# The second chunk's values ahead of five weight pieces, and the broadcast of the maxima moved to SyncE's queue

## The chip, the cores and the metric

The kernel runs on one core of a Trainium2 chip. The metric is device time in microseconds (us), taken on the core. A core has TensorE (PE, matrix products), VectorE (DVE), ScalarE (ACT), GpSimd (POOL) and SyncE (SP); SP, ACT and POOL can issue DMA transfers, and 16 DMA engines carry them. Each engine works through its own instructions in order and waits on semaphores for the others.

## The reference

An mLSTM cell over 4 batches x 8 heads, 768 steps, head width 40, and behind it a feed-forward block with 2048 hidden units:

```python
for t in range(S):
    m_new = np.maximum(f_gate[:, :, t] + m, i_gate[:, :, t])
    f_stab = np.exp(f_gate[:, :, t] + m - m_new)
    i_stab = np.exp(i_gate[:, :, t] - m_new)
    C = f_stab * C + i_stab * outer(vt, kt);  n = f_stab * n + i_stab * kt
    y[:, :, t] = sigmoid(o_gate[:, :, t]) * (C @ qt) / np.maximum(np.abs(n @ qt), 1.0)
x = y.transpose(0, 2, 1, 3).reshape(3072, 320)
h = x @ w_in                       # 320 x 2048
out = (h * sigmoid(1.702 * h)) @ w_out   # 2048 x 320
```

(Broadcast dimensions are shortened here.)

## The kernel before

The 768 steps are cut into six chunks of 128 steps (w = 0 to 5), and each chunk is worked in closed form: running maxima by scans on DVE (`gates`), weights between steps as exponentials on ACT (`weights`, L435), scores and values as matrix products (`scores`, `values`), and a state carried from chunk to chunk (`carry`, L596). While PE does the feed-forward block of chunk w, the attention part of chunk w+1 is put between its blocks. The order is written out by hand: the program is in manual schedule, so each engine and each DMA queue has exactly the order of the source.

The change concerns the time of chunk 0's feed-forward block (w = 0), about 25 to 110 us. These parts matter:

- *The pieces of the weights.* Both weight matrices arrive in 20 pieces of 128 x 512, 0 to 9 for w_in and 10 to 19 for w_out. `fetch(n)` (L157) issues the two or three DMAs of a piece on SP. `convert(n)` turns its bits into the form that PE reads: two activations on ACT (L243, L247) and four operations on DVE (L256, L257, L259, L265). `fetched` says at which pair of hidden blocks pieces are fetched, `converted` when they are converted: pieces 13, and 14 to 16, around the last two pairs; pieces 17, 18 and 19 at the output blocks 0, 4 and 5.
- *The up products.* `up(w, j, between)` (L608) does two of eight pairs of hidden blocks at a time, with j = 0, 2, 4, 6. ACT applies the activation (L635) to each pair, and runs the conversions between them.
- *The down products.* `down` (L753, matmuls on L758) is called in 16 blocks; the first eight use w_out's first half (pieces 10 to 14), the others the second half (pieces 15 to 19). After block 0 come `columns`, `scale` and `decay` of chunk 1, after block 1 and 3 `weights`, after block 3 `carry`, after block 6 `scores`, after blocks 8 and 9 `values`.
- *What a carry needs.* `scale` (L582, POOL) multiplies the values `v_st` of the chunk by factors in `cols` and writes `vw`; `carry` multiplies `vw` with k on PE. `cols` is filled by `columns` on ACT (L367, L371) from a small transposition on DVE (L356, `columns_turn`), which reads rows that went through DRAM (`gates`, `columns_in`).
- *The values.* `load(1, "v")` issues three DMAs on SP (L120): 320 KB and twice 160 KB, in runs of 40 numbers (160 bytes). `v_st` is one buffer, so chunk 1's values may be written only when chunk 0's were read by `values(0, 3)` and by `scale(0, 1)`.
- *The broadcast of the maxima.* `gates(1)` writes the running maxima to DRAM (`m_row`); `spread(1)` (L397) reads them back in four DMAs of 256 KB, each row spread to 64 partitions, into `wt`, where `weights` works on them. For w = 1 `side_queue` sends the small rows and this broadcast through POOL's queue, for later chunks through SP's.

A DMA of SP's queue is issued only when the one eight places before it has completed, as the program has eight semaphores in turn for them.

Of the kernel before, what the change touches and what calls it, by code (L numbers as in the profile page):

```python
# [26 lines left out]
def kernel(  # L27
# [12 lines left out]
    nc = tc.nc  # L40
# [12 lines left out]
    HL = L // 2  # L53
# [41 lines left out]
    def k_of(w):  # L95
        return (k_0, k_1)[w] if w < 2 else k_st[:, 0:BH * D].rearrange("s (h d) -> s h d", d=D)
# [13 lines left out]
    def load(w, what, bs=slice(0, B)):  # L110
        hs = slice(bs.start * H, bs.stop * H)
        for c in what:
            if c == "o" and w not in eo:
                eo[w] = ld.tile([L, BH, D], FP, tag="eo", bufs=1, name="eo")
            dst, src = {"k": (k_of(w), k), "q": (q_st, q), "v": (v_st, v), "o": (eo.get(w), o_gate)}[c]
            if w and c in "kv":
                for i, t, r in ((0, slice(0, L), slice(0, L)), (1, slice(0, HL), slice(HL, L)),
                                (1, slice(HL, L), slice(0, HL))):
                    x = src[:, :, w * L + t.start:w * L + t.stop, :].rearrange("b (p two) s d -> two s (b p) d", two=2)
                    nc.sync.dma_start(out=dst[r, i::2, 0:D], in_=x[i])  # L120
                continue
            nc.sync.dma_start(out=dst[:, hs, 0:D],
                              in_=src[bs, :, w * L:(w + 1) * L, :].rearrange("b h s d -> s (b h) d"))
# [109 lines left out]
    def convert(n):  # L233
        convert_begin(n)
        convert_end(n)
# [42 lines left out]
    def side_queue(w):  # L278

        return G if w == 1 else nc.sync  # L280
# [59 lines left out]
    def masks():  # L340
        V.tensor_reduce(out=odd, in_=full.rearrange("p (j two) -> p two j", two=2)[:, 1], axis=AX.X, op=OP.add)
        V.memset(odd[BH:2 * BH, :], 0.0)
        V.tensor_scalar(out=even, in0=odd, scalar1=-1.0, scalar2=1.0, op0=OP.mult, op1=OP.add)

    def columns_in(w):

        st_row, d_row = stacked[w]
        x = raw[w] = gate.tile([L, 5 * BH], FP, bufs=1, name="raw")
        for n in range(L // 32):
            side_queue(w).dma_start(out=x[n * 32:n * 32 + 32, 0:3 * BH].rearrange("r (k t) -> r k t", t=32),  # L350
                              in_=st_row[n].rearrange("(k r) t -> r k t", r=BH))
        side_queue(w).dma_start(out=x[:, 3 * BH:], in_=d_row.rearrange("h x -> (h x)").unsqueeze(0).to_broadcast([L, 2 * BH]))
# [44 lines left out]
    def spread(w):  # L397

        for c in range(2):
            x = wt[w, c] = work.tile([L, NJ, 2, HL], FP, tag="wt", bufs=2, name="wt")  # L400
            for n in range(2):
                src = m_row[w][n, c * PH:(c + 1) * PH].rearrange("h t -> (h t)")
                side_queue(w).dma_start(out=x[n * HL:(n + 1) * HL].rearrange("s j i t -> s (j i t)"),
                                  in_=src.unsqueeze(0).to_broadcast([HL, PH * HL]))

    p_w = {}
# [169 lines left out]
    def scale(w, c, part=0, parts=1):  # L576
        n = PH // parts
        hs = slice(c * PH + part * n, c * PH + (part + 1) * n)
        if part == 0:
            vw[w, c] = work.tile([L, PH, D1], FP, tag="u", name="vw")  # L580
        e = cols[w][:, 2 * BH + hs.start:2 * BH + hs.stop].unsqueeze(2).to_broadcast([L, n, D1])
        G.tensor_tensor(out=vw[w, c][:, part * n:(part + 1) * n], in0=v_st[:, hs, :], in1=e, op=OP.mult)  # L582

    def wait_for(x):

        G.tensor_copy(out=mark, in_=x[:, 0:1])

    def carry(w, c):
        js = slice(c * NJ, (c + 1) * NJ)
        pc = banks("p_c")  # L590
        n = 2 if 0 < w < NW - 1 else 1
        for j in range(NJ):
            for i in range(2):
                for x in range(n):
                    t = slot(i, x) if w else slice(0, L)
                    T.matmul(pc[i * 64:i * 64 + 64, x, j * D1:(j + 1) * D1], k_cols(w, t, c * PH + 2 * j + i),  # L596
                             vw[w, c][t, 2 * j + i, :], start=True, stop=True)
        new = lambda x: pc[:, x, 0:NJ * D1].rearrange("r (j d) -> r j d", d=D1)
        if w == 0:
            A.copy(out=state[1][:, js], in_=new(0))  # L600
            return
        for x, dst in enumerate((state_mid, state[1 - w % 2])[:n]):
            if x:
                decay(w, c, x, V)
            V.tensor_tensor(out=dst[:, js], in0=new(x), in1=dst[:, js], op=OP.add)
# [163 lines left out]
    def weight_sums(n):  # L769
        out, a, b = ((t1, w01, w00), (t2, w11, t1), (w01, w11, w01), (t4, w10, t2))[n]  # L770
        G.tensor_tensor(out=out, in0=a, in1=b, op=OP.subtract)
# [5 lines left out]
    def hidden_difference(w, j):  # L777

        a00, a10 = hidden(w, j, 0), hidden(w, j, 1)
        G.tensor_tensor(out=a10, in0=a00, in1=a10, op=OP.subtract)  # L780
# [51 lines left out]
    def run(calls):  # L832
        for f, *args in calls:
            f(*args)
# [47 lines left out]
    convert(2)  # L882

    converted = {0: ((3, 4), (5,)), 1: ((6,), (7, 8)), 2: ((9, 10), (11, 12)), 3: ((13,), (14, 15, None, 16))}
    fetched = {0: range(10, 18), 3: (18, 19)}

    def attention(w):
        at = (0, 1, 3, 3, 5, 6, 8, 8, 9, 12, 14) if w == 1 else (0, 0, 1, 3, 1, 4, 5, 6, 6, 10, 11)
# [9 lines left out]
    for w in range(NW):  # L898
        more = w + 1 < NW
        if w == 0:  # L900
            for j in range(NF // 2):
                if j % 2 == 0:
                    ahead, behind = converted[j // 2]
                    run([(convert, p) for p in ahead] + [(fetch, p) for p in fetched.get(j // 2, ())])
                    up(w, j, lambda: run([(columns_turn, 1) if p is None else (convert, p) for p in behind]))
                if j == 6:
                    load(1, "o")
                if j == 1:
                    wait_for(w_in_sb[:, 1, 512:1024])
                    scale(0, 1)  # L910
                if j < B and j % 2:
                    carry(0, j // 2)
                if j == 3:
                    masks()
                    gates(1)
                    columns_in(1)
                    spread(1)
                if j == 4:
                    load(1, "v")
                if j >= B:  # L920
                    transposes(1, j - B)
                if j in (4, 5):
                    block_transposes(1, 2 * j - 7)
        else:
            token_sums(w)
            if more:
                gates(w + 1)
                load(w + 1, "o")
            for j in range(NF // 2):
                up_fast(w, j)  # L930
                if w == 1 and j < 4:
                    weight_sums(j)
                if more and j == 2:
                    load(w + 1, "vk")
                    columns_in(w + 1)
                    spread(w + 1)
                if more and j:
                    for n in ((), (0, 2), (4,), (6, 1), (3,), (5, 7), ())[j - 1]:
                        block_transposes(w + 1, n)
                if more and j == 7:  # L940
                    columns_turn(w + 1)
                if 2 <= j < 6:
                    hidden_difference(w, j - 2)
                if j >= 6:
                    hidden_sums(w, (j - 6,), G)
            gelu_fast(w, NF // 2 - 1)
            hidden_sums(w, (2, 3), V)
        side = attention(w + 1) if more else {}
        if w == 0:
            block_transposes(1, 5)  # L950
            block_transposes(1, 7)

            blocks = [(lambda b=b, n=n: down(w, b, n)) for n0 in (0, 2) for b in range(B) for n in (n0, n0 + 1)]
        else:
            blocks = down_fast(w, 0) + down_fast(w, 1)
        for i, block in enumerate(blocks):
            if w == 0 and i in (0, 4, 5):
                convert((17, 18, 19)[max(i - 3, 0)])
            if w + 2 < NW and i == (6 if w == 0 else 0):
                load_gates(w + 2)  # L960
            if w + 2 < NW and i == 13:
                load_squares(w + 2, "kq" if w else "k")
            if w == 0 and i == 15:
                load_squares(w + 2, "q")
            block()
            run(side.get(i, []))
            if w == 0 and i in (11, 13):
                input_sums(slice(0, 4) if i == 11 else slice(4, 8))
# [30 lines left out]
```

## Time and profile before

| | |
|---|---|
| median of 3 runs | 468.26 us (467.49, 468.26, 473.1) |
| profiled execution, own time | 468.38 us |
| its span, first to last instruction | 466.7 us |
| PE busy | 459.5 us (98%) |
| DVE busy | 341.1 us (73%) |
| ACT busy | 189.3 us (41%) |
| POOL busy | 164.5 us (35%) |
| granted PE clock | 0.999 of full |
| DMA | 52.87 MB, 113 GB/s over the span |

A line of a timeline gives the start and the duration in us, the engine (a q behind it stands for the engine's queue of instructions, where DMAs are issued), the source line, what is written and read, the shape, and in brackets the idle time before and what ended it. A line of the waits gives the total, how often, and the longest, in us.

### The profile page before, as it was taken

How to read it: one execution, taken by the hardware profiler on the slowest of the kernel's cores; microseconds unless marked ns; L12 is line 12 of the kernel's file. 1: busy time of each engine (PE TensorE's matmuls, PEld its weight loads, DVE VectorE, ACT ScalarE, POOL GpSimd, SP SyncE). 2: the span in 40 equal slices, each digit the busy share in tenths (PEclk: the TensorE clock that was granted, in tenths of full speed). 3: DMA queues.
4: the chain of work that ended last, by engine and by line, in shares of the span. 5: the costliest groups of instructions: out<-in, count | busy, mean ns of one | idle time of the engine just before them, and what ended most of it. 6: DMA issues, size and time to landing. Idle time of an engine off the chain costs nothing.

```text
span 466.7 us, 12363 instructions
## 1 busy us (share of the span) xinstructions
PE 459.5 (98%) x5063; PEld 387.2 (83%) x5063; DVE 341.1 (73%) x699; ACT 189.3 (41%) x431; POOL 164.5 (35%) x157
## 2 busy tenths in 40 slices
PE   8999998999999999999999999999999999999997
PEld 6867875776778999678999778999878999876997
DVE  6788997789788876688875788876768867545612
ACT  5686699000536600554800453900444810254100
POOL 5101325200798600266800257610148510157100
PEclk9999999999999999999999999999999999999999
DMA  9999999038994045998024998114989305100000
GB/s 172 194 302 171 230 277 181 1 76 180 163 161 106 4 100 115 192 129 148 3 60 116 199 138 148 27 46 112 183 134 126 88 18 131 36 1 0 1 29 30
DMA packets 135561, 52.87 MB, mean 113 GB/s; under 512 B 101984, under 2 KB 131632, under 8 KB 135504
## 3 DMA queue, kind: packets, MB, share of 16 engines
q1 hardware_dynamic: 126816, 49.22, 55.9%
q10 hardware_dynamic: 8048, 1.66, 1.8%
q0 software_dynamic: 640, 1.20, 1.2%
q8 instruction: 40, 0.66, 0.6%
q14 instruction: 17, 0.14, 0.1%
HBM read 44.52 MB, written 7.54 MB: 112 GB/s over the span
## 4 chain that ended last, share of the span: by engine, by line
PE 94%; DMA 2%; DVE 1%; SPq 1%; issue 1%; POOL 0%; ACT 0%; POOLq 0%; DVEq 0%
PE p_out L812 33%; PE p_h L703 27%; PE p_h L711 8%; PE p_out L758 6%; PE p_h L620 5%; PE p_c L596 2%; DMA v_st<-in_v_dram 2%; PE p_o L503 2%; PE p_s L459 2%; PE p_i L511 2%; PE p_h L629 1%; PE p_t L386 1%; PE p_s L448 1%; SPq L120 1%; PE p_w L415 1%
## 5 line engine op out<-in xcount | busy, mean ns | idle before, releaser
L749 POOL TENSOR_TENSOR g<-g,parts 128x512 f32<-128x512 f32 x30 | 38.3, 1275 | 189.7 <-DVE parts L741 148.2
L737 ACT COPY parts<-p_h 128x256 f32<-128x256 f32 x40 | 14.9, 374 | 153.6 <-PE p_h L703 152.0
L812 PE MATMUL p_out<-w_out_sb,g 128*128 128x160 f32 x480 | 69.5, 301 | 0.0
L812 PEld LDWEIGHTS p_out<-w_out_sb,g 128*128 128x128 f32 x480 | 66.5, 190 | 0.9
L703 PE MATMUL p_h<-xT,w_in_sb 128*128 128x256 f32 x240 | 66.9, 388 | 0.0
L684 ACT ACTIVATE g<-g 128x512 f32<-128x512 f32 x80 | 50.0, 631 | 39.1 <-DVE g L744 24.5
L703 PEld LDWEIGHTS p_h<-xT,w_in_sb 128*128 128x128 f32 x240 | 43.7, 190 | 18.5 <-issue 6.7
L817 DVE TENSOR_TENSOR o_sb<-o_sb,p_out 128x160 f32<-128x160 f32 x70 | 21.4, 317 | 40.5 <-PE p_out L812 39.9
L812 PE MATMUL p_out<-t_sb,s 128*128 128x160 f32 x320 | 47.1, 300 | 0.0
L740 DVE TENSOR_TENSOR t_x<-p_h,parts 128x256 f32<-128x256 f32 x40 | 16.7, 418 | 39.0 <-PE p_h L711 34.2
L812 PEld LDWEIGHTS p_out<-t_sb,s 128*128 128x128 f32 x320 | 44.4, 190 | 0.2
L703 PE MATMUL p_h<-t_x,s_in 128*128 128x256 f32 x160 | 41.1, 379 | 0.0
L711 PE MATMUL p_h<-xT,w_in_x 64*128 64x512 f32 (+1 forms) x192 | 39.8, 540 | 0.0
L435 ACT ACTIVATE wt<-wt,cols 128x64 f32<-128x64 f32 x160 | 38.8, 333 | 0.1
L758 PE MATMUL p_out<-w_out_sb,g 128*128 128x320 f32 x128 | 35.7, 436 | 0.0
L703 PEld LDWEIGHTS p_h<-t_x,s_in 128*128 128x128 f32 x160 | 30.4, 190 | 4.1
L758 PEld LDWEIGHTS p_out<-w_out_sb,g 128*128 128x128 f32 x128 | 23.9, 190 | 9.6
L741 DVE TENSOR_TENSOR parts<-p_h,t_x 128x512 f32<-128x512 f32 x40 | 27.7, 692 | 3.5
L620 PE MATMUL p_h<-xT,w_in_sb 128*128 128x256 f32 x128 | 29.8, 385 | 0.0
L748 ACT COPY g<-p_h 128x512 f32<-128x512 f32 x30 | 17.4, 580 | 30.7 <-PE p_h L711 25.3
L711 PEld LDWEIGHTS p_h<-xT,w_in_x 64*128 64x128 f32 x192 | 16.9, 186 | 14.7 <-issue 13.5
L744 DVE TENSOR_TENSOR g<-p_h,parts 128x512 f32<-128x512 f32 x40 | 27.6, 691 | 1.4
(198 smaller groups left out, 840.1 us busy)
## 6 DMA issues: line engine op xcount, KB each, us to landing
q_sq<-in_q_dram SPq DMA_DIRECT2D x20, 320.0 KB, 10.3
k_sq<-in_k_dram SPq DMA_DIRECT2D x16, 320.0 KB, 6.4
wt<-m_row SPq DMA_DIRECT2D x16, 256.0 KB, 5.2
out_dram<-o_sb SPq DMA_DIRECT2D x24, 160.0 KB, 2.0
eo<-in_o_gate_dram SPq DMA_DIRECT2D x5, 640.0 KB, 7.5
bits<-in_moe_w_in_dram SPq DMA_DIRECT2D x6, 512.0 KB, 9.9
q_sq<-x_row SPq DMA_DIRECT2D x10, 256.0 KB, 2.9
v_st<-in_v_dram SPq DMA_DIRECT2D x14, 160.0 KB, 5.3
```

Of the source, the lines that this page charges most:

```text
L435: A.activation(out=x[:, h, :], in_=x[:, h, :], func=AF.Exp, scale=-1.0, bias=cols[w][:, c * PH + h:c * PH + h + 1])
L620: T.matmul(ph[j][i][:, t], w_in_sb[:, c, f * 128:(f + 1) * 128], x[:, c, t], start=(first and c == 0 and n == 0), stop=(not first and c == ...
L684: A.activation(out=gs[w, j][:, i, :], in_=gs[w, j][:, i, :], func=AF.Gelu_apprx_sigmoid)
L703: T.matmul(out, a, x[n], start=start, stop=stop)
L711: T.matmul(row[:, t], w_in_x[r, j, :], rest_x[r, 2, t], start=(not late and h == 0), stop=(late and h == n - 1))
L741: V.tensor_tensor(out=y[:, half_w:3 * half_w].rearrange("p (a t) -> p a t", a=2), in0=flat[:, half_w:3 * half_w].rearrange("p (a t) -> p a ...
L744: V.tensor_tensor(out=g[:, 1, :], in0=row1, in1=y[:, half_w:3 * half_w], op=OP.add)
L748: A.copy(out=g[:, 0, :], in_=row0)
L749: G.tensor_tensor(out=g0, in0=g0, in1=u, op=OP.add)
L758: T.matmul(po, gs[w, f // 2][:, f % 2, b * L:(b + 1) * L], w_out_sb[:, f, :], start=(f == 0), stop=(f == NF - 1))
L812: T.matmul(po, a(f), b[:, f, :], start=(f == 0), stop=(f == NH - 1))
L817: V.tensor_tensor(out=dst, in0=x, in1=po, op=OP.add)
```

## The change

Three edits. The load of the second chunk's values (`load(1, "v")`) is issued at j = 1, right behind `scale(0, 1)`, instead of at j = 4. Of the pieces that were fetched together at the first pair (10 to 17), pieces 13 to 17 are fetched at the second (j = 2), so that the values stand between piece 12 and piece 13 in SP's queue. The broadcast (`spread`) is issued by SP for every chunk, and for chunk 1 at j = 4 instead of j = 3; it stands in SP's queue between piece 17 and piece 18. POOL keeps the small rows of chunk 1 (`m_row`, `st_row`, `d_row`, `raw`). On PE, DVE and ACT the instructions and their order are the same.

```diff
@@ spread
-                side_queue(w).dma_start(out=x[n * HL:(n + 1) * HL].rearrange("s j i t -> s (j i t)"),
+                nc.sync.dma_start(out=x[n * HL:(n + 1) * HL].rearrange("s j i t -> s (j i t)"),
                                   in_=src.unsqueeze(0).to_broadcast([HL, PH * HL]))
@@ the order of chunk 0
-    fetched = {0: range(10, 18), 3: (18, 19)}
+    fetched = {0: range(10, 13), 1: range(13, 18), 3: (18, 19)}
...
                 if j == 1:
                     wait_for(w_in_sb[:, 1, 512:1024])
                     scale(0, 1)
+                    load(1, "v")
                 if j < B and j % 2:
                     carry(0, j // 2)
                 if j == 3:
                     masks()
                     gates(1)
                     columns_in(1)
+                if j == 4:
                     spread(1)
-                if j == 4:
-                    load(1, "v")
```

## The prediction

> **What bounds the kernel now.** I read the page first (busy times, slices), then the list of waits for the stretch that the change touches, then the chain of waits there, and last the timelines of ScalarE (ACT) and SyncE (SP).
>
> ```profile
> span 466.7 us, 12363 instructions
> ...
> PE 459.5 (98%) x5063; PEld 387.2 (83%) x5063; DVE 341.1 (73%) x699; ACT 189.3 (41%) x431; POOL 164.5 (35%) x157
> ...
> DMA  9999999038994045998024998114989305100000
> ```
>
> TensorE (PE) is busy 459.5 of 466.7 us, so no reordering can win more than the 7.2 us left, 1.5%. The first seven DMA digits are 9: up to about 80 us the DMA engines are full. There a load can only come earlier if another comes later. The waits between 58 and 95 us:
>
> ```profile
> POOL vw L582 <- DMA v_st<-in_v_dram: 11.4, 1, 11.4
> ...
> PE p_c L596 <- POOL vw L582: 2.1, 2, 1.6
> POOL wt L403 <- DMA raw<-st_row: 2.0, 1, 2.0
> ```
>
> PE loses 2.1 us here (1.57 + 0.55) before the two carries of the second chunk, because GpSimd (POOL) scales the values late, and POOL waits for the load of v. The chain, start and duration in us:
>
> ```profile
> 64.05 10.94 DMA v_st<-in_v_dram
> ...
> 75.16 0.17 POOL vw L582
> ...
> 76.44 1.74 POOL vw L582
> 78.18 0.04 issue
> 78.22 1.14 PE p_c L596 x64
> ```
>
> After 78.2 the chain is PE to the end of the kernel, so what is won or lost here reaches the end whole. The timeline of ACT shows what else a carry needs (start, duration):
>
> ```profile
> 58.95 0.70 ACT L243 ACTIVATE w_out_sb<-bits 128x512 f32<-128x512 f32 x1
> 59.54 0.68 ACT L247 ACTIVATE bits<-bits 128x512 uint32<-128x512 uint32 x1
> 60.98 1.08 ACT L635 ACTIVATE g<-p_h 128x512 f32<-128x512 f32 x2 [0.77 <-PE p_h L629]
> ...
> 69.87 0.26 ACT L367 ACTIVATE cols<-cols 128x64 f32<-128x64 f32 x1
> 70.03 0.51 ACT L371 ACTIVATE cols<-raw 64x32 f32<-64x32 f32 x2
> 70.57 0.59 ACT L435 ACTIVATE wt<-wt,cols 128x64 f32<-128x64 f32 x2
> ```
>
> 58.95 is the conversion of piece 13, the first of those that the change puts behind v. From there to the scale factors (cols, 70.13) ACT idles once, for 0.77 us. POOL's scaling reads both v and cols: v came at 74.99, cols 4.9 us before it.
>
> **The change, part by part.** (1) The three loads of v move from behind pieces 13 to 17 (12 DMAs) to in front of them. SP issued the last part of piece 12 at 49.2 and the first of piece 13 at 51.4; a DMA of SP waits for the completion of the one eight places ahead. So v is issued from 51.4 instead of 59.7. What v overwrites was last read by POOL's earlier scaling, done at 37.0, and by PE at 23.4: no new wait.
>
> When does v land? The engines are full, so it is served after piece 12, whose last part lands at 49.2 + 6.6 = 55.8. Its service time has two bounds. Low: the k load of the same shape and line (L120) landed at 43.7, behind gate rows that landed at 38.0: 5.7 us. High: v in this trace, from piece 17's landing (58.5 + 6.0 = 64.5) to 75.0, is 10.4 us, with 1 MB of broadcast reads (4 x 256 KB on POOL's queue) inside; at the 354 GB/s of the window 59 to 64 us those are 3.0 us, which leaves 7.4. I take 6.5, between 5.7 and 7.4, as the broadcast is no longer beside it: v lands at 62.3, 12.7 us earlier than now.
>
> The Trainium skill's page "DMA: Bandwidth & Descriptors" (section "Anatomy of one DMA — SWDGE (gpsimd) path") fits 2.0 us plus bytes over 436 GB/s, an estimate of 3.5 us for these 640 KB; v would land at 59.3, and the sum would be the full gain of the second case below. [...]
>
> (2) Pieces 13 to 17 come later. Piece 18 stands behind v now, in the same three parts as piece 13, and its last part lands at 71.5 + 4.8 = 76.3, 1.3 us after v. So piece 13 is complete at 62.3 + 1.3 = 63.6; today it is at 52.5 + 4.7 = 57.2, with 1.7 us in hand before ACT's 58.95. ACT now waits at the conversion until 63.6, and behind it in ACT's order stand the activations of pair 6, pieces 14 to 16, pair 7, the copies of kT, piece 17, cols, and the exponentials of L435. From 58.95 to 70.13 these are 11.18 us, less the 0.77 of idle time that the delay swallows: 10.4. For waits inside (piece 16 is issued only after v has landed, and 62.3 + 4.7 + two more parts is about 68, just when ACT gets there) I allow 0.5, between 0 and 1.5. Cols are done at 63.6 + 10.4 + 0.5 = 74.5, 4.4 later than now.
>
> (3) So POOL's scaling starts at 74.5, released by ACT instead of by v. One scaling took 1.3 us (75.16 to 76.44): the first carry can start at 75.8 instead of 76.5; PE has been ready since 74.96. The second follows as now. **Gain 0.7 of the 2.1 us.** Break-even is piece 13 at 64.3; past it each us of lateness costs one.
>
> (4) VectorE (DVE) is released by ACT's first half of piece 13, at 64.2 instead of its own 62.3. A piece takes it 2.35 us (62.27 to 64.61), so 13 and 14 are done at 68.9. PE's second output block starts at 68.4 (66.18 + 8.78/4) and reaches piece 14 half-way, at 69.5: 0.6 in hand. A stall there is the same lateness as in (3), not more, as the carry waits for cols anyway.
>
> (5) The four broadcast reads of L403 leave POOL, where they took 0.5 us each to issue while POOL had nothing else until 75.2: worth nothing. On SP they stand behind piece 17 and in front of pieces 18 and 19, o and the gates. Later chunks show them on SP: 3.05 us for four issues, 5.2 us from issue to landing. Issued at about 67 to 69, behind a full queue, they land at 72 to 74; ACT's L435 starts at 74.9. Hidden, with about 1 us of cover and more behind it (third rival). POOL's small rows keep their place, and the columns they bring are turned by DVE (69.3 now) about 2 us later, ahead of ACT's cols. Pieces 18 and 19, needed after L435 (74.9 + 7.75 = 82.7), land by about 80 with the same total traffic. Nothing is added to or removed from any engine's work.
>
> The sum goes by one profiled execution: 468.38 us, span 466.7 and 1.7 around it, 0.1 above the median of 468.26. 468.38 - 0.7 = 467.7; against the median **467.6**.
>
> **The rivals.** *The cover holds* and the stall goes whole: piece 13 complete by about 62.6, cols at 73.0, both scalings in time. 468.26 - 2.1 = 466.2. For it: with k's 5.7 us piece 13 comes at 62.8. Against it: the v row itself, and the queue that refills behind v (piece 16).
>
> *Piece 13 late, slower.* In ACT's order everything behind its conversion is late, and cols take v's place as the last thing, later than v was. It decides from 64.3. With the high bound, 10.4 us for v, piece 13 comes at 55.8 + 10.4 + 1.3 = 67.5 and cols at 77.9 to 78.4: the carry at 79.2 to 79.7, 2.7 to 3.2 later than now, 471.0 to 471.5; half-way 469.7. For it: ACT sits 4.6 us before the first w_out piece already, so these loads have no large lead, and SP's issue of v was held for 3.5 and 4.5 us. Against it: the 10.4 holds broadcast traffic that moves away.
>
> The page "TensorE: Matmul & The Clock Gate" (Part 1) says that PE's clock halves after some 3.4 us idle. The present wait of 1.57 us shows a granted clock of 1.00 in its stretch, which the page allows; a wait of 4.7 us would bring by it about 2 us more, an estimate of mine, to 473.
>
> *The broadcast late, slower.* The reads land behind pieces 13 to 17. L435 (7.75 us), two pieces on ACT and DVE and the product with the scores (1.2) must be over by PE's 92.55; the product ended at 89.9. Counting 7.75 + 0.7 + 4.9 to 6.8 + 1.2 back from 92.55, L435 must start by 76.1 to 78.0. At the longest landing on POOL's queue, 8.7 us after an issue at 69, it would start at 77.7: 0 to 1.6 lost besides the missed gain, 468.3 to 469.9. Against it: 5.2 us is the usual time.
>
> That the change does nothing, v landing at 75 again, would need v held back at issue; nothing ahead of it in SP's queue waits past 52.
>
> **How the numbers follow.** Forecast (gain 0 to 1.4) 0.43; full gain 0.22; piece 13 late 0.25; broadcast late 0.07; no effect 0.03. The likeliest gives 467.6, its own range 466.8 to 468.4. To hold 8 in 10 the range takes in the full gain with 0.2 of scatter, 466.0, and most of the late case, 471.0. A measurement of this kernel tells about 2% (9.4 us) from no change. Faster by that is more than PE's whole idle time: 0.01. Slower by it needs late pieces, a late broadcast and a slowed PE together: 0.04. Within: 0.95.
>
> **What would show it.** In the profile after: v lands near 62; POOL's wait before L582 ends by ACT's L367, not by the DMA of v; ACT has a new wait of about 4.6 us before L243, ended by the DMA of bits; L435 starts near 75; PE's wait at L596 is 0.5 to 1.5 us instead of 2.1. Wrong would be: no wait on ACT (the full gain), a wait at L758 for pieces of w_out, an L435 that waits for its broadcast, or a wait at L596 over 2.1.

## The result and the profile after

| | before | after |
|---|---|---|
| median of 20 runs each, on one chip | 468.6 us (466.26 to 473.1) | 468.1 us (466.65 to 470.55) |
| ratio after to before, 95% interval | | 0.9991 [0.9967, 1.0015] |
| profiled execution: time, span | 468.38, 466.7 us | 467.52, 465.8 us |

No change that can be measured: the medians are 0.5 us apart, and the interval reaches from 1.5 us won to 0.7 lost. The page of the changed kernel:

```profile
span 465.8 us, 12359 instructions
...
PE 459.9 (99%) x5063; PEld 387.9 (83%) x5063; DVE 340.9 (73%) x699; ACT 189.3 (41%) x431; POOL 163.9 (35%) x153
...
DMA  8999998049993036997024998024999305000000
```

The span is 0.9 us shorter, PE's busy time is the same within 0.4, and the DMA engines are full as before, up to about 80 us. The list of waits between 58 and 95 us of the changed kernel (total, how often, longest):

```profile
POOL vw L582 <- DMA wt<-m_row: 13.1, 1, 13.1
ACT w_out_sb L243 <- DMA bits<-in_moe_w_out_dram: 3.8, 1, 3.8
DVE u L517 <- PE p_i L511: 3.0, 1, 3.0
```

ACT has the new wait for piece 13 that the forecast spoke of. PE's wait before the carries (L596) is gone from the list. The name behind POOL's wait is not its cause: the scaling L582 reads `v_st` and `cols`, not the broadcast. It began when ACT had just written `cols`, as the timelines of ACT and POOL show (start, duration):

```profile
57.09 1.07 ACT L388 COPY kT<-p_t 128x512 f32<-128x512 f32 x2
61.98 0.68 ACT L243 ACTIVATE w_out_sb<-bits 128x512 f32<-128x512 f32 x1 [3.82 <-DMA bits<-in_moe_w_out_dram]
...
72.26 0.26 ACT L367 ACTIVATE cols<-cols 128x64 f32<-128x64 f32 x1
72.96 7.76 ACT L435 ACTIVATE wt<-wt,cols 128x64 f32<-128x64 f32 x32
```

```profile
72.65 2.65 POOL L582 TENSOR_TENSOR vw<-v_st,cols 128x656 f32<-128x656 f32 x2 [13.11 <-DMA wt<-m_row]
```

`cols` (L367) ends at 72.52, the scaling starts at 72.65, and both halves are done at 75.30. PE gets to the carry after that, at 75.96, as the chain of waits shows (start, duration):

```profile
67.34 8.62 PE p_out L758 x32
75.96 2.01 PE p_c L596 x128
77.96 6.66 PE p_out L758 x24
```

The carry runs without a gap. The blocks behind it start at 77.96 instead of 79.36: 1.4 us earlier, of which 0.9 is left at the end. Of the rest 0.3 goes at 148 us, where PE's weight load (L812) waits for an activation of ACT as it did not before, and 0.2 behind PE's last matmul.

The removed wait was 2.1 us, and the start of PE's down products was 1.0 later in this execution than in the one before (67.18 against 66.18), by no instruction that the change moved on PE. So the phase of one execution, that is, how far PE and the DMA queue have come by this place, matters as much as the effect, and more profiles were taken.

### The profile page after: what moved, and what is told of

Read it like the earlier page. It is cut to its first block, busy times and chain, and to the rows that moved or that the text cites. A ratio compares the mean times of both kernels' runs of the same rounds, so it can differ in the third digit from the quotient of the medians.

```text
span 465.8 us, 12359 instructions
## 1 busy us (share of the span) xinstructions
PE 459.9 (99%) x5063; PEld 387.9 (83%) x5063; DVE 340.9 (73%) x699; ACT 189.3 (41%) x431; POOL 163.9 (35%) x153
## 4 chain that ended last, share of the span: by engine, by line
PE 94%; SPq 1%; DVE 1%; POOL 1%; DMA 1%; ACT 0%; issue 0%; DVEq 0%
PE p_out L812 33%; PE p_h L703 25%; PE p_h L711 8%; PE p_out L758 8%; PE p_h L620 6%; PE p_c L596 3%; PE p_o L503 2%; PE p_s L459 2%; PE p_i L511 2%; PE p_h L629 2%; PE p_t L386 1%; PE p_s L448 1%; SPq L120 1%; DMA k_sq<-in_k_dram 1%; PE p_o L493 0%; PE p_w L415 0%
## 5 line engine op out<-in xcount | busy, mean ns | idle before, releaser
L812 PE MATMUL p_out<-w_out_sb,g 128*128 128x160 f32 x480 | 69.6, 301 | 0.1
L812 PEld LDWEIGHTS p_out<-w_out_sb,g 128*128 128x128 f32 x480 | 66.5, 190 | 1.2 <-ACT g L684 0.4
L812 PE MATMUL p_out<-t_sb,s 128*128 128x160 f32 x320 | 47.2, 300 | 0.0
L812 PEld LDWEIGHTS p_out<-t_sb,s 128*128 128x128 f32 x320 | 44.4, 190 | 0.2
L435 ACT ACTIVATE wt<-wt,cols 128x64 f32<-128x64 f32 x160 | 38.8, 333 | 0.1
L758 PE MATMUL p_out<-w_out_sb,g 128*128 128x320 f32 x128 | 35.7, 436 | 0.0
L758 PEld LDWEIGHTS p_out<-w_out_sb,g 128*128 128x128 f32 x128 | 23.9, 190 | 9.5
## 6 DMA issues: line engine op xcount, KB each, us to landing
q_sq<-in_q_dram SPq DMA_DIRECT2D x20, 320.0 KB, 10.2
bits<-in_moe_w_in_dram SPq DMA_DIRECT2D x6, 512.0 KB, 10.5
```

Of the source, the lines that this page charges most:

```text
L435: A.activation(out=x[:, h, :], in_=x[:, h, :], func=AF.Exp, scale=-1.0, bias=cols[w][:, c * PH + h:c * PH + h + 1])
L758: T.matmul(po, gs[w, f // 2][:, f % 2, b * L:(b + 1) * L], w_out_sb[:, f, :], start=(f == 0), stop=(f == NF - 1))
L812: T.matmul(po, a(f), b[:, f, :], start=(f == 0), stop=(f == NH - 1))
```

## The experiments

The theories were these. A (the forecast): v no longer comes last; piece 13 comes late on ACT instead, so `cols` sets the carry and most of the gain is given back; the broadcast's move is worth nothing by itself. The rival: the broadcast's move matters as much as that of v. B, in the expectations of b2 and a2: the wait is the same in every execution of a kernel, and the change loses some 1.5 us at another place. C, formed after the first repeats: a wait of PE costs more than its length, as its clock falls behind it. Each ratio is to runs of the kernel before on the same chip in the same session; the medians of before were 469.14 (29 runs), 467.95 (30) and 469.23 (32).

**Both kernels again** (b2 and b3 the kernel before, a2 and a3 the changed one; no edit).

> The kernel before, unchanged, profiled a second time. Theory A (phase): PE and the DMA queue reach this place with a lead that differs by 1 to 2 us from run to run (in the two profiles so far PE began its down blocks at 66.18 and 67.18, and piece 12 landed at 55.8 and 54.0), so the wait of PE at L596, 2.1 us in the first profile, will be another one here, between 0 and 4 us, equal to (v's landing + about 1.5) minus PE's arrival. Theory B (given back): the wait is 2.1 within 0.3 in every run of this kernel, and the change loses about 1.5 us at another place. Ratio to itself 1.000 within 0.003 under both.

> The changed kernel, profiled a second time. Theory A (phase): v lands about 6.4 us and piece 13 about 7.9 us after the last part of piece 12; ACT waits at L243 for piece 13, 3 to 5.5 us; PE waits at L596 only if piece 13 + 10.7 + 1.3 is later than PE's arrival: 0 to 1 us. Ratio to before 0.996 to 1.000. Theory B (given back): no wait at L596, and a wait of 1 us or more of PE at a place behind it that the profile of before has not.

> The kernel before, profiled a third time, after waits of 2.1 and 2.6 us at L596. Theory A (phase): a wait between 0 and 3 us, ended by v's landing; theory C: a lowered clock behind it only if the wait is over 2 us in one piece. Rival: exactly 2.1 to 2.6 again. Ratio to itself 1.000 within 0.004.

> The changed kernel, profiled a third time. The first profile had no wait at L596 and the second 1.8 us. Theory A (phase): piece 13's landing against PE's arrival decides; a wait between 0 and 2 us, ended by ACT's cols whenever it is there, and never by the load of v. Median 467.5 to 469, ratio to before 0.996 to 1.001.

Ratios: b2 1.0008 [0.9971, 1.0045], b3 0.9982 [0.9945, 1.0019], which is the scatter of a kernel against itself; a2 0.9992 [0.996, 1.0023], a3 0.9977 [0.9946, 1.0008]. With the first run, three profiles of each kernel (us):

| | PE's down products start | v lands | piece 13 complete | PE's wait at L596 | clock behind it | time |
|---|---|---|---|---|---|---|
| before | 66.18 | 74.99 | 57.2 | 1.57 + 0.55 | 1.00 | 468.38 |
| b2 | 66.66 | 76.46 | 58.78 | 2.64 | 0.50 | 472.09 |
| b3 | 67.04 | 75.76 | 57.84 | 1.82 + 0.55 | 0.50 | 472.46 |
| after | 67.18 | 60.41 | 61.88 | 0 | 1.00 | 467.52 |
| a2 | 67.15 | 62.50 | 64.13 | 1.54 + 0.28 | 1.00 | 469.99 |
| a3 | 66.31 | 62.18 | 63.56 | 0.44 + 0.11 | 1.00 | 467.46 |

The waits (58 to 95 us) of a2 and then of a3 show the mechanism of A without the accident of the first profile:

```profile
POOL vw L582 <- ACT cols L367: 16.0, 1, 16.0
ACT w_out_sb L243 <- DMA bits<-in_moe_w_out_dram: 6.2, 3, 4.7
...
PE p_c L596 <- POOL vw L582: 1.8, 2, 1.5
```

```profile
POOL vw L582 <- ACT cols L367: 13.9, 1, 13.9
ACT w_out_sb L243 <- DMA bits<-in_moe_w_out_dram: 5.4, 1, 5.4
```

POOL is released by ACT's `cols`, ACT waits 4.7 to 5.4 us for piece 13 (in a2 two more waits for later pieces follow it), and PE waits for POOL: 1.8 in a2, 0.55 in a3. (For a2 0 to 1 had been expected; the two further waits on ACT, 1.5 us, are the difference.) Theory B is not borne out: the wait is another one in each execution of both kernels, and from the end of the carries to PE's last matmul a2 and a3 lose nothing against the first profile of before.

b2 shows something that the first profile of before did not: the clock falls. Its PE timeline, and its stretches (window, length, busy us and instructions of PE, PE's weight loads, DVE, ACT, POOL, then the granted clock, the DMA share and GB/s):

```profile
78.08 3.65 PE L596 MATMUL p_c<-vw,t_sb 64*64 64x41 f32 x128 [2.64 <-POOL vw L582]
81.66 8.06 PE L758 MATMUL p_out<-w_out_sb,g 128*128 128x320 f32 x24
```

```profile
76.00:77.00 1.00, 0.00 (x0) 0.00 (x0) 0.74 (x2) 1.00 (x5) 0.38 (x1) 1.00 0.79 269
77.00:78.00 1.00, 0.00 (x0) 0.00 (x0) 0.00 (x0) 1.00 (x5) 1.00 (x2) 0.78 1.06 337
78.00:79.00 1.00, 0.92 (x36) 0.92 (x38) 0.00 (x0) 1.00 (x6) 1.00 (x2) 0.50 0.72 190
...
84.00:85.00 1.00, 1.00 (x5) 0.69 (x4) 0.96 (x3) 1.00 (x2) 0.94 (x2) 0.81 0.02 2
```

The clock is 1.00 as the wait begins and 0.50 when PE resumes. The means of the rows 77 (0.78) and 84 (0.81) put the changes at 77.56 and 84.38, so it is at 0.50 for 6.8 us. The carries take 3.65 us and the 24 matmuls behind them 8.06; at full clock (swap, below) the same two lines have 2.08 and 6.73. That is 2.9 us on top of a wait of 2.64. In b3 the clock fell the same way behind 1.82 + 0.55, where C had expected it only behind more than 2 us in one piece.

**The broadcast alone** (e_s): issued by SP, behind piece 17 and ahead of v; pieces and v as before.

```diff
-                side_queue(w).dma_start(
+                nc.sync.dma_start(
...
-                    spread(1)
                 if j == 4:
+                    spread(1)
                     load(1, "v")
```

> Only the broadcast moved to SyncE's queue, behind piece 17 and in front of v; v stays where it was. Theory A: the same bytes are served in front of v whether beside it or ahead of it; v lands within 1 us of where it did in the kernel before (10.4 us after piece 17), PE's wait at L596 is that of the kernel before, about 2 us, and the time is that of before within 0.3%. Rival (the queue matters: the broadcast out of GpSimd's queue lets v through sooner, or SyncE's issue of v comes 3 us later and v with it): v 3 us earlier and no wait, or 2 to 3 us later and a wait of 4 to 5 us.

468.75 us, 0.9972 [0.9941, 1.0003]. v landed at 75.05, and PE's wait was there as before:

```profile
PE p_c L596 <- POOL vw L582: 2.6, 2, 2.0
```

So the broadcast's queue alone, with its 1 MB still in front of v, does not take PE's wait away.

**The values alone** (e_v): pieces and v as in the changed kernel, the broadcast left on POOL's queue at j = 3.

```diff
-    fetched = {0: range(10, 18), 3: (18, 19)}
+    fetched = {0: range(10, 13), 1: range(13, 18), 3: (18, 19)}
...
                     scale(0, 1)
+                    load(1, "v")
...
-                if j == 4:
-                    load(1, "v")
```

> The values moved as in the change, the broadcast left on GpSimd's queue and at its old place. Theory A: the load of v alone carries the change. v lands before 62, as the broadcast is issued only from about 60; the broadcast then shares the engines with pieces 13 to 17, which land up to 3 us later (piece 13 less than 1 us later); ACT waits in all 4 to 6 us at L243; PE's wait at L596 0 to 1 us. Ratio to the changed kernel 1.000 within 0.003. Rival (the broadcast's move matters as much): PE's wait at L596 stays at 1.5 us or more.

476.29 us, 1.0146 [1.0102, 1.0191]: 7 us slower than before. A missed this. The rival had it that the broadcast matters, but not the place: it expected 1.5 us or more at L596, where PE waits 0.5. The ACT timeline and PE's waits of e_v:

```profile
67.48 0.66 ACT L243 ACTIVATE w_out_sb<-bits 128x512 f32<-128x512 f32 x1 [7.80 <-DMA bits<-in_moe_w_out_dram]
...
73.20 0.66 ACT L243 ACTIVATE w_out_sb<-bits 128x512 f32<-128x512 f32 x1 [3.54 <-DMA bits<-in_moe_w_out_dram]
```

```profile
PE p_out L758 <- ACT g L635: 2.4, 1, 2.4
PE p_out L758 <- DVE w_out_sb L265: 2.0, 1, 2.0
```

Piece 13 was complete at 67.37 and piece 14 at 73.12; a2, whose piece 12 landed at the same time (56.24, here 56.41), had them at 64.13 and 67.43. PE's down products wait twice: the gelu of pair 6 (L635) stands behind piece 13 on ACT and frees, by the code, the bank that the first down product writes; later they wait for a late piece. The granted clock was 0.58 from 70 to 74 us and 0.50 from 78 to 80, which makes the two waits dearer still; all six runs of e_v have a lowered mean clock (0.989 to 0.993). What takes the pieces' time is in the DMA view of e_v from 56 to 76 us (queue: packets, MB, share of the 16 engines; then issues: count, KB each, median us to landing):

```profile
q1 hardware_dynamic: 3813, 2.71, 63.1%
q0 software_dynamic: 504, 1.14, 27.3%
...
bits<-in_moe_w_out_dram SPq DMA_DIRECT2D x5, 320.0 KB, 11.0
wt<-m_row POOLq DMA_DIRECT2D x4, 256.0 KB, 9.2
```

POOL's queue, nearly all of it the broadcast, held 27.3% of the engines for 20 us, as much as the whole of them for 5.5 us, and the parts of the pieces took 11.0 us to land instead of 6.7 in the changed kernel. The Trainium skill's page "DMA: Bandwidth & Descriptors" (section "Queues, rings and completion order") says that each DMA engine takes its queues in turn, packet by packet; e_v fits this, as a 1 MB read issued at 61.3 to 65.3 held up pieces that SP had issued beside it.

**Piece 13 ahead of v** (mid), against the changed kernel:

```diff
-    fetched = {0: range(10, 13), 1: range(13, 18), 3: (18, 19)}
+    fetched = {0: range(10, 14), 1: range(14, 18), 3: (18, 19)}
```

> The changed kernel with piece 13 ahead of v, so that v stands between pieces 13 and 14. Theory A: ACT meets its wait at piece 14 instead of 13; as pair 6's activations lie between them, the wait is about 1 us shorter than in the changed kernel's second profile (6.2 us in all at L243, 1.8 us of PE's wait at L596): 4 to 5.5 us on ACT, 0 to 1 us at L596, no lowered clock. v lands 1.5 us later, without effect. Ratio to before 0.994 to 1.000. Rival (v's landing sets the carry, not ACT): PE's wait at L596 grows by 1 us or more.

468.27 us, 1.0003 [0.9976, 1.0031]. The waits of mid:

```profile
ACT w_out_sb L243 <- DMA bits<-in_moe_w_out_dram: 3.4, 3, 1.7
...
PE p_c L596 <- POOL vw L582: 0.7, 2, 0.5
```

Piece 13 was there at 56.34, and ACT waited for the pieces behind v instead, three times, 3.4 us in all (4 to 5.5 had been expected, and a ratio of at most 1.000); L367 started at 73.66, between the 72.26 of the changed kernel's first profile and a3's 73.80. The lateness is that of all the pieces behind v, not of the first one.

**More bytes ahead of piece 13** (late), against the changed kernel: chunk 1's output gates, 640 KB, go with v.

```diff
-                if j == 6:
-                    load(1, "o")
...
-                    load(1, "v")
+                    load(1, "vo")
```

> The changed kernel with the output gates of chunk 1 (640 KB, the same 160-byte runs) also ahead of piece 13. Theory A, slope: piece 13 lands 6 to 6.5 us later than in the changed kernel, at 68 to 71; ACT waits at L243 10 us or more; each us past break-even (piece 13 at about 64 to 65) costs PE one: 4 to 6 us of waits, part at L758 for piece 14, part at L596, and by theory C a stretch at a clock of 0.50 that costs 2 to 4 us more. Time 473 to 478, ratio to before 1.010 to 1.020. Rival (the pieces have cover enough, and the change's effect is of v alone): within 0.3% of the changed kernel.

472.38 us, 1.0082 [1.0049, 1.0115]: slower, by somewhat less than expected. The waits of late:

```profile
ACT w_out_sb L243 <- DMA bits<-in_moe_w_out_dram: 8.4, 1, 8.4
...
PE p_out L758 <- ACT g L635: 1.5, 1, 1.5
PE p_c L596 <- POOL vw L582: 0.7, 1, 0.7
PE p_out L758 <- DVE w_out_sb L265: 0.3, 1, 0.3
```

Piece 13 was complete at 66.75, less late than I had thought. Its profiled execution (470.77 us, clock 1.00) is one of three of its seven at 470.6 to 470.8 us and a mean clock of 0.998 or 1.00; the other four have 0.995 or 0.996 and 472.4 to 473.4. The profiled one shows the waits alone: its span is 469.0, 2.3 us over that of before. By the forecast's break-even (64.3, and each us later costs one) it should be 2.45; that the two agree so well is in part chance, as single executions differ by 1 to 2 us in phase. Of PE's 2.5 us of waits 0.7 are at the carry and 1.8 at L758, 1.5 of these for the gelu, which the forecast had left out.

**The gap filled** (warm): the kernel before, with ten matmuls of zeros (L191, results unused) ahead of the first carry, so that PE does not stand idle.

```diff
+    def fill(w):
+        if w == 1:
+            keep_busy(10, banks("p_fill")[:, 0, :])
...
-                 [(weights, w, 0)], [(weights, w, 1)], [(carry, w, 0), (carry, w, 1)], ...
+                 [(weights, w, 0)], [(weights, w, 1)], [(fill, w), (carry, w, 0), (carry, w, 1)], ...
```

> The kernel before with ten short matmuls of zeros (L191, about 2.2 us together) on PE right in front of the first carry, where PE would wait; they write a bank that nothing reads. Theory C (the granted clock): in the second profile of before a wait of 2.64 us at L596 was followed by 6.5 us at a clock of 0.50, about 3 us of time, where the first profile's 1.57 us was not. So the slow half of before's runs are those with the longer wait. With the matmuls in the gap the clock stays at 1.00, nothing on the path is added (the wait was 2.1 to 2.6 us), and the runs over 470.5 us are gone: median 467.5 to 468.7, ratio 0.994 to 0.999, and no run above 471. Rival (the spread of before comes from elsewhere, start-up or memory): the spread and the median stay, ratio 1.000 to 1.005.

469.47 us (468.42 to 470.55), 1.0026 [1.0002, 1.0049], above the expected median. The PE timeline of warm:

```profile
74.81 2.32 PE L191 MATMUL p_fill<-t_sb 128*128 128x512 bf16 x10
77.06 2.08 PE L596 MATMUL p_c<-vw,t_sb 64*64 64x41 f32 x128
```

The wait is gone and its time is not: the fill costs 2.3 us in every execution, also in those that would have waited less. The ratio is the rival's, the narrower spread C's: all 12 runs have a mean clock of 0.999 or 1.00 and none is over 470.55; of the 30 runs of before beside them 5 have 0.993 to 0.996, those from 470.4 up. That fits C, but is too few to tell.

**A longer wait** (delay): the order of swap below, with POOL's scaling of one half done six times over.

```diff
-        G.tensor_tensor(out=vw[w, c]..., in0=v_st[:, hs, :], in1=e, op=OP.mult)
+        for _ in range(6 if (w, c) == (1, 0) else 1):
+            G.tensor_tensor(out=vw[w, c]..., in0=v_st[:, hs, :], in1=e, op=OP.mult)
```

> The version with the pieces in the order of before and the broadcast on SyncE behind v (no wait at L596), with GpSimd's first scaling of the second chunk done six times instead of once, the same result each time: five more of about 1.3 us in front of the carry, which then comes about 6.5 us later than 71.8: PE waits about 3 us at L596, and for nothing else. Theory C (the clock): such a wait is followed by about 6.5 us at a granted clock of 0.50, so the time goes up by the wait and about 3 us more: 472.5 to 474.5, where that version alone has 467.0. Rival (a wait costs its length and no more): 469.5 to 470.7 and a clock of 1.00 throughout.

474.31 us, 1.01 [1.0066, 1.0134]; in the same session the same order without the repeats took 467.03, 7.3 us less. The PE timeline of delay, whose lines are one further down, and its row of the granted clock in 40 slices:

```profile
80.75 3.65 PE L597 MATMUL p_c<-vw,t_sb 64*64 64x41 f32 x128 [4.97 <-POOL vw L583]
84.34 8.74 PE L759 MATMUL p_out<-w_out_sb,g 128*128 128x320 f32 x24
```

```profile
PEclk9999997799999999999999999999999999999999
```

The wait is 4.97 us, longer than expected. Behind it the carries take 1.6 us more and the 24 matmuls 2.0 more than in swap, at a clock of 0.50 from 78.2, within the wait, to 88.4 us: 8.6 us in all, of the 9.4 between the profiled executions of delay and swap2 (475.75 and 466.38). All nine runs have a mean clock of 0.989 to 0.996. C holds for such a wait: it costs its length and then the slower clock.

**Pieces and v in the old order, the broadcast on SP behind v** (swap, and again as swap2).

```diff
-                side_queue(w).dma_start(
+                nc.sync.dma_start(
...
-                    spread(1)
                 if j == 4:
                     load(1, "v")
+                    spread(1)
```

> The pieces and v in the order of before, the broadcast on SyncE behind v instead of on GpSimd beside it. If ACT's order is what late pieces act through (theory A), nothing of ACT's chain is late here: cols at 70 to 71 as before, v alone is served behind piece 17 and lands about 6.5 us after it (71 to 73), the scaling ends 1.5 us later, and PE's wait at L596 is 0 to 0.5 us, without a lowered clock: ratio to before 0.994 to 0.998. The price: the broadcast lands 3 us after v, L435 waits 3 to 5 us for it and starts at 73 to 76. Rival (the broadcast late): L435's lateness goes on through pieces 18 and 19 and the product with the scores, PE waits 1.5 us or more at L503, ratio 1.000 or above.

> The pieces and v in the order of before, the broadcast on SyncE behind v, a second time and beside the changed kernel. Theories A and C together: neither v nor cols is late at the carry, so no wait at L596 and a narrow spread (within 1.5 us), median 466.5 to 467.5, 0.3 to 0.4% below the changed kernel. Rival (its first result was a lucky draw of the start): spread and median those of the changed kernel.

466.98 us (466.48 to 467.66), 0.998 [0.996, 1.0], and 467.03 us (466.38 to 468.27), 0.9941 [0.9915, 0.9968]. PE in swap, and swap's waits:

```profile
75.08 2.08 PE L596 MATMUL p_c<-vw,t_sb 64*64 64x41 f32 x128
77.09 6.73 PE L758 MATMUL p_out<-w_out_sb,g 128*128 128x320 f32 x24
```

```profile
POOL vw L582 <- ACT cols L367: 9.6, 1, 9.6
...
ACT wt L435 <- DMA wt<-m_row: 1.1, 1, 1.1
```

Piece 17 landed at 64.94 and v at 69.60, 4.7 us later, where the first profile of before had 10.4. `cols` were written from 70.07, the scaling began at 70.46 with v there, and no carry waited. The broadcast landed last, at 70.67 to 75.60; ACT waited 1.1 us for its first part, which nothing behind it felt. So what made v too late for the carry was the broadcast and not the five pieces in front of it: with the broadcast beside v or ahead of it (before, b2, b3, e_s), v lands at 75.0 to 76.5; with it behind v (swap, swap2, delay), at 69.4 to 71.6. swap has the lowest median of all, and its 24 runs lie within 1.9 us, none with a lowered clock; all 135 of before have a standard deviation of 2.0 us, the 44 of the changed kernel 1.3.

## Why the prediction was right

- *The time.* 467.6 was forecast, 468.1 measured, inside the likeliest case's own range. In the three comparisons the medians of the changed kernel lie 0.5, 0.2 and 0.4 us below those of before, against 0.7 forecast; pooled, 468.5 (44 runs) and 468.8 (135, b2 and b3 among them). The sign of so small a gain is not settled by the medians; that it is small is. That the medians come so near the forecast is in part luck: the term that it rests on, PE's wait at the carry, is another one in each execution.
- *Steps 1 to 3* held as terms. v landed 6.4, 6.3 and 7.5 us after piece 12 (6.5 forecast; the 3.5 us that the prediction set beside it is short of all three); piece 13 was complete 1.5, 1.6 and 1.4 after v (1.3); ACT waited 3.8, 4.7 and 5.4 at L243 (4.6); from there to the end of L367 it took 10.5, 12.2 (with 1.5 of further waits) and 10.4 (10.9). What failed is what the terms were added to. Piece 12 landed at 53.99, 56.24 and 54.69 where the forecast had 55.8 from one execution, and PE reached the carry at 75.96 in the first profile, not 74.96. A gain of 0.7 is smaller than these shifts, so the wait is 0, 1.8 or 0.55 and not one number. The first profile looked like the rival of the full gain; a2 is the case in which the carry is late; a3 lies between, the only one inside the 0.5 to 1.5 us that the forecast named.
- *The size of the broadcast* was wrong. The forecast took 3.0 us for its 1 MB, by the rate of another window. Beside other loads it costs near twice that: e_v's share of the engines gives 5.5 us, and v's 10.4 in the first profile of before less swap's 4.7 gives 5.7. Served in order on SP's queue, from piece 17's landing to its own, it took 4.2 to 4.4 in the three profiles of the changed kernel and in e_s, still well over 3.0. The stretches of the changed kernel show why the rate did not carry over:

```profile
64.00:66.00 2.00, 2.00 (x11) 1.77 (x10) 1.83 (x4) 2.00 (x5) 0.00 (x0) 1.00 1.07 374
...
70.00:72.00 2.00, 2.00 (x9) 1.39 (x8) 1.93 (x5) 1.98 (x3) 0.00 (x0) 1.00 1.05 235
```

  Full engines move 374 GB/s of pieces, but 235 while the broadcast is among them. With 5.5 the forecast's own subtraction would have given 4.9 for v at its old place without the broadcast (4.7 to 5.1 in swap, swap2 and delay), and so the cheaper cure that swap is.
- *Step 5*, that the broadcast's move is worth nothing, was wrong for this reason. It looked at POOL's time to issue, and at the landing on SP's queue, but not at what the broadcast does to the pieces that the change had just put beside it: left on POOL's queue it costs 1.5%. On SP, behind piece 17, it landed at 70.3 to 73.5 (72 to 74 forecast) and L435 started at 72.96, hidden as forecast. So the move of v needs that of the broadcast to come out even; the broadcast's own move (e_s, 0.9972) comes out even without it.
- *Step 4* (DVE's cover of 0.6 us) held: the first profile has no wait at L758, a2 a wait of 0.17 there. What it left out, that L758 also waits for the gelu behind piece 13 on ACT, sets the price once piece 13 is later than here (late, e_v).
- *The clock* was priced only for waits near 4.7 us, and not for the kernel before. The Trainium skill's page "TensorE: Matmul & The Clock Gate" (Part 1) gives some 3.4 us idle, counted in windows that run freely, before the clock halves. Here it halved after 2.64 (b2) and 1.82 + 0.55 (b3), and did not after 2.02 + 0.55 (e_s) or 1.57 + 0.55 (before): the waits that tripped it are shorter than the page's figure, and the length of the wait alone does not decide, as e_s and b3 show. The traces do agree with the windows: counted from the first clock record of an execution, the clock changes only at whole multiples of 3.41 us (it was at 0.50 for 3.41 twice in e_v, 6.83 in b2 and b3, 10.24 in delay). In the window just before each fall PE was idle for 1.82 (b3), 2.01 and 1.98 (e_v), 2.12 (b2) and 2.42 us (delay); of the windows between 60 and 95 us that ran at 1.00 and no fall followed, in all the profiles here, the idlest had 1.76 (e_s), 1.45 (late) and 1.36 (before). So about half a window was enough, and not only the length of a wait counts but how much of it falls into one window; no run was made to test this.
- *What the change did win* the forecast had no term for. The mean granted clock over the span is on record for every run but the first 20 of before. Of the other 115 of before, all 40 over 470.0 us have 0.989 to 0.996, and all 75 under it 0.999 or 1.00; 3.41 us at 0.50 make about 0.996 of a span of 470, and 6.83 about 0.993. Of the changed kernel's 44 runs one is lowered (a3's slowest, 471.45, 0.995); two of a2 are over 471 at a clock of 1.00, which stays unexplained. So the change took away most of the runs with a fallen clock, 40 in 115 against 1 in 44 (35 in 85 against 1 in 24 in the two later sessions that had both kernels), while among the runs at full clock its median is not lower (468.3 against 468.0). The shorter waits of its profiles (0, 1.8 and 0.55 against 2.1 to 2.6) are the likely reason; in which stretch the clock fell is seen only where a run was profiled.

Open is why the queue's and PE's phases shift by 1 to 2 us between executions, and why e_s, with the waits of before in its profile, has a lowered clock in only 1 of its 12 runs.

## What to carry to other kernels

When a load is late on full DMA engines, look at what shares the engines with it, on any queue, and first move back what is not due soon: here the broadcast, due last, cost v 4 to 6 us, while moving v ahead of five pieces only made the pieces late. Price a transfer by the share of the engines that its queue held in the trace, not by its bytes at another transfer's rate. And where the effect is smaller than the phase between queues, read several profiles of the same kernel before adding terms to one of them, and the granted clock of every run: medians 0.3 us apart hid a clock that fell in a third of the runs of one kernel and almost never in the other.

## What the runs showed of the hardware

- A PE wait of 2.64 us cost 5.5 us (b2: 2.64 and 2.9 for the slower clock), one of 4.97 cost 8.6 (delay). The clock was at 0.50 for 6.8 us in b2 and 10.2 in delay, from within the wait on.
- The clock changed only on a grid of 3.41 us. Between 60 and 95 us it fell behind windows of this grid in which PE was idle for 1.82 us or more (b3, e_v, b2, delay) and behind none with 1.76 or less (e_s, late, before, and the other profiles). The ends of matmuls are modelled in a trace, so the idle times are, too.
- Two queues share the engines: the 320 KB parts of pieces took 11.0 us from issue to landing beside the broadcast (e_v), 6.7 without it (the changed kernel).
- The broadcast's 1 MB, which reads the same few rows for 64 partitions each, took 4.2 to 4.4 us in order on SP's queue and 5.5 beside the pieces, 1.5 to 2 times its bytes at the pieces' rate (1.05 MB at 374 GB/s would be 2.8).
